# Threshold attention and its feed-forward block on one core: centring behind the masks, the last quarter product ahead of the next scores, the variance in a slot's second half

## The chip, the cores and the metric

The kernel runs on one core of a Trainium2 chip. The metric is the time on the device in microseconds (us), the median of several runs. A core has five engines that run side by side and wait for each other through semaphores: TensorE (PE in the profile, its weight loads PEld), VectorE (DVE), ScalarE (ACT), GpSimd (POOL) and SyncE (SP), which issues most transfers here.

## The reference

Eight batches, eight heads, 576 positions, head size 64. Attention keeps only scores that lie within `tau` of their row's maximum; a feed-forward block (FFN) with layer norm and a residual follows.

```python
scores = scale * q @ k.T                       # (8, 8, 576, 576)
thresh = max(scores, -1) - tau
scores = where(scores >= thresh, scores, -1e9)
attn   = exp(scores - max(scores, -1));  attn /= sum(attn, -1) + 1e-9
x      = attn @ v                              # heads side by side: (8, 576, 512)

mu  = mean(x, -1);  var = mean((x - mu) ** 2, -1)
xn  = (x - mu) / sqrt(var + 1e-6) * g_ln
out = x + relu(xn @ w_ch1) @ w_ch2             # 512 -> 2048 -> 512
```

All inputs and the output are float32.

## The kernel before

The attention of a batch is cut into 9 **slots**, 72 in all. A slot computes the scores of four blocks of 128 rows, their maxima, exponentials, masks and sums, and turns the weights over by way of DRAM; the product with the values follows a slot later. The FFN runs on 16 **groups** of 288 positions, two per batch, and fills TensorE's time between the attention's products. Every slot has four **quarters**, 0 to 3; a call can be hung on a quarter, and each quarter has a quota of FFN steps.

The heart of a slot. The engines take instructions in the order in which this loop issues them:

```python
for n in range(NS):                       # NS = 72
    scores(b, s); run(n, -1)              # TensorE -> sc[0], sc[1] in PSUM
    rest = exponentials(n)                # DVE maxima (L399), ACT exp of blocks 0 and 1 (L410)
    es, thr = next(rest)
    run(n, 0); ...; second_part(n, 0)     # quarter 0
    next(rest, None)                      # ACT exp of blocks 2 and 3
    ...                                   # transposes of the next q and k, where due
    run(n, 1); second_part(n, 1)          # quarter 1
    diags = weights(es, thr, blocks_go)   # DVE masks with row sums (L417), POOL scaling (L433)
    run_all(aside); drip(); ...
    run(n, 2); second_part(n, 2)          # quarter 2
    scr = turn_blocks(s, es)              # DVE block transposes (L498), et -> scr in DRAM
    at_quarter(n + 1, 0, ...fetch...)     # scr -> em
    at_quarter(n + 1, 3, ...values_of...) # TensorE, L542, into pv_behind
    if s in (HP, 2 * HP): group_ready(2 * b + (s > HP))
    run_all(aside); drip({nc.vector: 4, nc.gpsimd: 6}); ...
    run(n, 3); ...; second_part(n, 3)     # quarter 3
    run_all(aside); drip({nc.vector: 2, nc.gpsimd: 0})
```

`pv_behind`, where the value products go, lies behind the two score blocks in `sc[0]`, in the last of its three banks. `aside` and `drops` hold short vector work (root steps, sums, output stores) that is issued between quarters.

When a group's input is complete, three calls are hung up: its mean (a product with a matrix of 1/512), the centring, and the start of its FFN steps.

```python
def ready(g):
    if g < 2: return (24, 42)[g]
    b, t = divmod(g, 2)
    return QUARTERS * (b * SLOTS + (HP, 2 * HP)[t] + 2) + (2, 4)[t]

def group_ready(g):
    first = divmod(ready(g), QUARTERS)
    for fn in (mean_of, centre):
        at_quarter(*(divmod(ready(g) - 1, QUARTERS) if g else (first[0], -1)), fn, g)
    at_quarter(*first, lambda: queue.append(ffn_steps(g)))

def mean_of(g):
    if banks_taken[0]:
        waiting_mean.append(g)            # no bank free: the last quarter product issues it
        return
    means[g] = ps_ff.tile([128, TOK], F32, tag="ff", name="mean")
    product(means[g], lhsT=avg_sb, rhs=sums.pop(g), start=True, stop=True)

def centre(g):
    nonlocal issued, owed
    while waiting_mean:                   # draws FFN steps until the mean is out
        cost = next(queue[0])[1]
        issued += cost
        owed -= cost
    xc = centred[g] = ffn.tile([128, NK, TOK], F32, tag="xc", bufs=1, name="xc")
    for c in range(NK):                   # four DVE subtractions, L593
        nc.vector.tensor_tensor(out=xc[:, c], in0=groups[g][:, c], in1=mean, op=ALU.subtract)
```

So the first group of a batch (g even) is ready in quarter 2 of slot 6 of its batch and the second (g odd) in quarter 0 of slot 2 of the next; the mean and the centring are hung one quarter earlier. Group 1 is ready in quarter 2 of slot 1 of batch 1. The pool `ps_ff` has two banks, for all FFN products, means and variances.

The quota. `issued` counts FFN steps by cost, `owed` is what a quarter still has to issue:

```python
ROOM = (0.6, 1.0, 1.25, 0.35)

def second_part(n, i):
    at = QUARTERS * n + i
    g = sum(issued >= e for e in ends)
    left = sum(ROOM[t % QUARTERS] for t in range(at, ready(g + 1))) if g + 1 < NG else 0
    owed += (ends[g] - issued) * ROOM[i] / left if left > 0 else 8
    got = 1 if i in (0, QUARTERS - 1) else 2
    while queue and (owed >= 0.5 or got == 1 and i in (0, QUARTERS - 1)):
        got, cost = next(queue[0], (None, 0))
        ...
        issued += cost; owed -= cost
```

The steps of a group: 16 rows of four products (`p1`, 128x288, cost 1 each) with a relu after each row; on the way the square, the variance and the reciprocal root. Then, for all groups but the first, seven quarter products (`seg`, 16 steps of cost 0.5 each, two products of 128x144 per step), the last of them in the bank that the mean waits for.

```python
def first_part(g):
    for d in range(ND):                                     # ND = 16
        while d == ND - 2 and len(rooted) <= g: run_all(aside)
        p1 = ps_ff.tile([128, TOK], F32, tag="ff", name="p1")
        for c in range(NK): product(p1, ...); ... yield 1, 1
        nc.scalar.activation(hidden[:, d], p1, func=AF.Relu)            # L716
        if sq is None and d and (plain or part > 1 or d == ND // 2 - 1):
            squared = d
            sq = hidden[:, ND - NK :]
            nc.scalar.activation(sq, xc, func=AF.Square)                # L722, then 3 POOL sums
        elif sq is not None and rb is None and d >= squared + (7 if plain else 4) and (part or d == ND - NK - 1):
            var = ps_ff.tile([128, TOK], F32, tag="ff", name="var")
            product(var, lhsT=avg_sb, rhs=sq[:, 0], start=True, stop=True)
            rb = ffn.tile([128, TOK], F32, tag="rb", bufs=2, name="rb")
            nc.scalar.activation(sq[:, 2], var, func=AF.Identity, bias=eps_sb)
            aside.append(lambda: root(rb, sq[:, 2], sq[:, 3]))
            yield 1, 1

def root(y, x, t, step=0):                                  # DVE, on 128x288
    if step == 0: ... first guess (L650)
    ... three instructions of a Newton step (L654, L657, L658)
    if step < 2: aside.append(lambda: root(y, x, t, step + 1))
    else: rooted.append(y)

def second_quarters(g, rb):
    banks_taken[0] = True
    ... six segments ...
    last = segment(s4, b22)
    for _ in range(12): yield next(last)
    banks_taken[0] = False
    while waiting_mean: mean_of(waiting_mean.pop(0))
    p3 = yield from last                                    # 4 more steps, then a copy on ACT (L797)
```

Of the kernel before, what the change touches and what calls it, by code (L numbers as in the profile page):

```python
# [18 lines left out]
def kernel(  # L19
# [37 lines left out]
    NK = DM // 128  # L57
    ND = DF // 128
# [37 lines left out]
    def product(out, lhsT, rhs, **flags):  # L96


        for h in range(2):
            r = slice(64 * h, 64 * h + 64)  # L100
            nc.tensor.matmul(out[r], lhsT=lhsT[:, r], rhs=rhs, **flags)  # L101
# [480 lines left out]
        product(means[g], lhsT=avg_sb, rhs=sums.pop(g), start=True, stop=True)  # L582

    def centre(g):
        nonlocal issued, owed
        while waiting_mean:
            cost = next(queue[0])[1]
            issued += cost
            owed -= cost
        xc = centred[g] = ffn.tile([128, NK, TOK], F32, tag="xc", bufs=1, name="xc")  # L590
        mean = means.pop(g)
        for c in range(NK):
            nc.vector.tensor_tensor(  # L593
                out=xc[:, c], in0=groups[g][:, c], in1=mean, op=ALU.subtract
            )
# [4 lines left out]
    aside, stores, drops = [], [], []  # L600
# [17 lines left out]
    def run_all(calls):  # L618
        now = calls[:]
        calls.clear()  # L620
        for fn in now:
            fn()
# [23 lines left out]
    def root(y, x, t, step=0):  # L646


        if step == 0:
            nc.vector.tensor_scalar(  # L650
                out=y.bitcast(I32), in0=x.bitcast(I32), scalar1=-0.5, scalar2=float(0x5F3759DF),
                op0=ALU.mult, op1=ALU.add,
            )
        nc.vector.scalar_tensor_tensor(  # L654
            out=t, in0=y, scalar=-0.5, in1=y, op0=ALU.mult, op1=ALU.mult
        )
        nc.vector.tensor_mul(t, t, x)  # L657
        nc.vector.scalar_tensor_tensor(out=y, in0=t, scalar=1.5, in1=y, op0=ALU.add, op1=ALU.mult)  # L658
        if step < 2:
            aside.append(lambda: root(y, x, t, step + 1))  # L660
        else:
            rooted.append(y)

# [10 lines left out]
    def differences():  # L674


        flat = conversion.stage.rearrange("p a b -> p (a b)")
        flat4 = e_room[1].rearrange("p a b -> p (a b)")
        size = HM * HD * 128
        for t in (flat[:, :size], flat[:, size : 2 * size], flat4[:, :size]):  # L680
            more.append(t.rearrange("p (m d c) -> p m d c", m=HM, d=HD))
        s2, s3, s4 = more
        s1 = w2[1, 0]
        for eng, out, a, b, op in (
            (nc.gpsimd, s3, w2[0, 0], w2[1, 0], ALU.subtract),
            (nc.vector, s1, w2[1, 0], w2[1, 1], ALU.add),
            (nc.vector, s2, s1, w2[0, 0], ALU.subtract),
            (nc.gpsimd, s4, w2[0, 1], s2, ALU.subtract),
        ):
            for m in range(HM):  # L690
                for d in range(0, HD, 4):
                    at = (slice(None), m, slice(d, d + 4))
                    eng.tensor_tensor(out=out[at], in0=a[at], in1=b[at], op=op)
                    yield

    def first_part(g):


        xc = centred.pop(g)
        rb = sq = None  # L700
        plain = g == 0
        sums_of = differences() if g == 1 else iter(())
        for d in range(ND):
            while conversion.ended < 4 * (d // 4 + 1):
                yield 0, 0
            while d == ND - 2 and len(rooted) <= g:
                run_all(aside)
            p1 = ps_ff.tile([128, TOK], F32, tag="ff", name="p1")
            for c in range(NK):
                product(  # L710
                    p1, lhsT=w1_sb[c][:, d * 128 : (d + 1) * 128], rhs=xc[:, c],
                    start=(c == 0), stop=(c == NK - 1),
                )
                if c < NK - 1:
                    yield 1, 1
            nc.scalar.activation(hidden[:, d], p1, func=AF.Relu)  # L716
            next(sums_of, None)
            yield 2, 1
# [3 lines that stand above are left out]
                nc.scalar.activation(sq, xc, func=AF.Square)  # L722
                for c in range(1, NK):
                    nc.gpsimd.tensor_tensor(out=sq[:, 0], in0=sq[:, 0], in1=sq[:, c], op=ALU.add)
            elif sq is not None and rb is None and d >= squared + (7 if plain else 4) and (part or d == ND - NK - 1):

                var = ps_ff.tile([128, TOK], F32, tag="ff", name="var")
                product(var, lhsT=avg_sb, rhs=sq[:, 0], start=True, stop=True)
                rb = ffn.tile([128, TOK], F32, tag="rb", bufs=2, name="rb")
# [3 lines that stand above are left out]
        for _ in sums_of:  # L733
            pass
        return rb
# [118 lines left out]
    def ffn_steps(g):  # L854
        rb = yield from first_part(g)
        yield from (second_quarters if g else second_plain)(g, rb)
# [3 lines left out]
    QUARTERS = 4  # L860
# [5 lines left out]
    queue = []  # L866
    issued = part = now = 0
    owed = 0.0
    later_calls = {}

    def at_quarter(n, i, fn, *args):
        later_calls.setdefault((n, i), []).append((fn, args))
# [5 lines left out]
    def ready(g):  # L878

        if g < 2:  # L880
            return (24, 42)[g]
        b, t = divmod(g, 2)
        return QUARTERS * (b * SLOTS + (HP, 2 * HP)[t] + 2) + (2, 4)[t]
# [25 lines left out]

    def group_ready(g):  # L910
        first = divmod(ready(g), QUARTERS)
        for fn in (mean_of, centre):
            at_quarter(*(divmod(ready(g) - 1, QUARTERS) if g else (first[0], -1)), fn, g)
        at_quarter(*first, lambda: queue.append(ffn_steps(g)))

    conversion = Weights()
# [16 lines left out]
    for n in range(NS):  # L933
# [58 lines left out]
        if s in (HP, 2 * HP):  # L992
            group_ready(2 * b + (s > HP))
# [51 lines left out]
```

## Time and profile before

| | |
|---|---|
| time, median of 3 runs | 1425.12 us (1424.98 to 1427.36) |
| span of the profiled execution | 1420.1 us |
| granted TensorE clock | 0.993 |
| busy: PE, DVE, POOL, ACT | 94%, 67%, 43%, 32% |
| products `p` (L101) | 4096 records, 519.6 us busy |
| products `seg` (L101), all forms | 5760 records of the two large groups, 369.0 us busy |
| masks (L417) | 288 of 810 ns |
| maxima (L399) | 144 of 1351 ns |
| block transposes (L498) | 112 of 1371 ns |
| centring (L593) | 64, median 447 ns |

A group's row in the profile names line, engine, operation, output and inputs, shape and count, then busy time and the mean duration of one, then the idle time of the engine just before and what ended it. L101 is the helper `product`, so its groups go by tiles: `p` is a row of the first FFN product, `seg` a quarter product, `mean` and `var` the two averages. A product of this helper is two half matmuls, and each stands as two records, so four records are one product. `<-` after a gap names what the engine waited for. A timeline line gives start, duration (of merged instructions together), engine, line, operation, tiles, count, and in brackets the gap ahead of it.

### The profile page before, as it was taken

Reading aid. Unit: us, or ns where it says so; the run is one execution under the profiler, and the core shown is the slowest. Engines: PE = TensorE matmul, PEld = TensorE weight load, DVE = VectorE, ACT = ScalarE, POOL = GpSimd, SP = SyncE. Lnnn points to the kernel's source line nnn. Section 1 sums busy time; section 2 is a strip of 40 time slices with the busy share of each in tenths; the row PEclk is TensorE's granted clock in tenths of the full one; section 3 lists DMA queues with packets and bytes.
Section 4 is the critical chain, followed back from the end, with each engine's and each line's share of the span. In section 5 each row is a group of like instructions: output and inputs, shape, how many; then the busy total and the mean of one; then the engine's idle time right before and its main releaser. Section 6 shows DMA issues by size and latency. Waiting matters only on the chain.

```text
span 1420.1 us, 36022 instructions
## 1 busy us (share of the span) xinstructions
PE 1341.9 (94%) x15048; PEld 985.7 (69%) x15048; DVE 950.0 (67%) x1638; ACT 459.1 (32%) x923; POOL 612.0 (43%) x809
## 2 busy tenths in 40 slices
PE   4878999999999999999999999999999999999996
PEld 3655665857767595866768586776858677685866
DVE  5998958576776677666775767766675677757221
ACT  3887513232222323232232322323232322223120
POOL 2445444544534354353443544343544444434312
PEclk8999999999999999999999999999999999999998
DMA  9622456557864687557875678646875577555211
GB/s 230 170 75 84 90 134 165 156 159 154 186 148 125 164 181 169 156 141 167 182 161 137 155 156 176 153 133 167 187 163 154 142 163 174 144 134 150 68 18 18
DMA packets 466867, 205.53 MB, mean 145 GB/s; under 512 B 275024, under 2 KB 428368, under 8 KB 466704
## 3 DMA queue, kind: packets, MB, share of 16 engines
q1 hardware_dynamic: 461936, 202.64, 59.7%
q8 instruction: 118, 1.93, 0.6%
q10 hardware_dynamic: 4736, 0.59, 0.4%
q14 instruction: 45, 0.37, 0.1%
q0 software_dynamic: 32, 0.00, 0.0%
HBM read 119.41 MB, written 83.76 MB: 143 GB/s over the span
## 4 chain that ended last, share of the span: by engine, by line
PE 73%; DVE 13%; DMA 5%; ACT 3%; issue 3%; POOL 1%; SPq 1%; POOLq 0%; DVEq 0%; ACTq 0%
PE p L101 29%; PE seg L101 24%; PE sc L385 9%; PE sc L542 9%; DVE e L417 3%; DMA em<-scr 3%; DVE neg L399 3%; ACT e L410 1%; DVE xc L593 1%; DMA scr<-et 1%; DVE w L291 1%; DVE w L264 1%; DVE y L801 1%; PE mean L101 0%; PE tp L101 0%
## 5 line engine op out<-in xcount | busy, mean ns | idle before, releaser
L101 PE MATMUL p<-xc,w 128*64 128x288 f32 x4096 | 519.6, 408 | 19.7 <-ACT hidden L716 9.2
L101 PEld LDWEIGHTS p<-xc,w 128*64 128x64 f32 x4096 | 288.9, 137 | 231.2 <-ACT hidden L716 20.1
L399 DVE TENSOR_REDUCE neg<-sc 128x2 f32<-128x1152 f32 x144 | 188.7, 1351 | 209.4 <-PE sc L385 209.4
L410 ACT ACTIVATE e<-sc,neg 128x576 f32<-128x576 f32 x288 | 196.3, 742 | 244.1 <-DVE neg L399 244.1
L433 POOL TENSOR_SCALAR e<-e,den 128x576 f32<-128x576 f32 x252 | 196.3, 790 | 181.9 <-DVE den L422 181.9
L101 PE MATMUL seg<-hidden,w 128*64 128x144 f32 x3840 | 245.7, 287 | 0.0
L101 PEld LDWEIGHTS seg<-hidden,w 128*64 128x64 f32 x3840 | 235.0, 137 | 8.9 <-issue 6.3
L417 DVE SCALAR_TENSOR_TENSOR e<-sc,thr,e 128x576 f32<-128x576 f32 x288 | 222.1, 810 | 22.4 <-ACT e L410 21.9
L716 ACT ACTIVATE hidden<-p 128x288 f32<-128x288 f32 x256 | 105.4, 413 | 237.1 <-PE p L101 236.2
L403 POOL TENSOR_SCALAR thr<-neg,low_sb 128x2 f32<-128x2 f32 x144 | 42.0, 292 | 321.9 <-DVE neg L399 311.9
L385 PE MATMUL sc<-kT,qT 64*128 64x384 f32 (+3 forms) x1024 | 150.6, 425 | 21.6 <-DVE qT L345 10.1
L498 DVE STREAM_TRANSPOSE et<-e 128x1152 f32<-128x1152 f32 x112 | 152.3, 1371 | 11.5 <-POOL e L433 9.6
L385 PEld LDWEIGHTS sc<-kT,qT 64*128 64x128 f32 x1024 | 94.3, 191 | 73.2 <-issue 19.6
L542 PE MATMUL sc<-em,v_in 128*64 128x256 f32 (+1 forms) x1408 | 131.6, 330 | 10.9 <-DVE e L417 5.6
L101 PE MATMUL seg<-hidden,stage 128*64 128x144 f32 x1920 | 123.3, 286 | 0.0
L101 PEld LDWEIGHTS seg<-hidden,stage 128*64 128x64 f32 x1920 | 118.3, 137 | 3.1 <-issue 2.3
L542 PEld LDWEIGHTS sc<-em,v_in 128*64 128x64 f32 x1408 | 85.6, 137 | 47.6 <-DVE e L417 9.1
L782 POOL TENSOR_TENSOR hidden<-hidden 128x576 f32<-128x576 f32 x60 | 84.6, 1429 | 29.5 <-ACT hidden L716 19.6
L559 ACT COPY x<-sc 128x256 f32<-128x256 f32 x60 | 22.3, 372 | 213.5 <-PE sc L542 176.7
L568 POOL TENSOR_TENSOR sum<-sum,x 128x256 f32<-128x256 f32 (+1 forms) x64 | 32.3, 504 | 105.4 <-ACT x L559 102.9
L782 DVE TENSOR_TENSOR hidden<-hidden 128x576 f32<-128x576 f32 x60 | 47.9, 832 | 40.3 <-PE seg L101 37.3
L797 ACT COPY part<-seg 128x288 f32<-128x288 f32 x75 | 30.1, 401 | 115.3 <-PE seg L101 111.0
(151 smaller groups left out, 1204.8 us busy)
## 6 DMA issues: line engine op xcount, KB each, us to landing
scr<-et SPq DMA_DIRECT2D x252, 288.0 KB, 4.6
em<-scr SPq DMA_DIRECT2D x63, 1024.0 KB, 5.9
out_dram<-ot SPq DMA_DIRECT2D x256, 36.0 KB, 2.7
q_in<-in_q_dram SPq DMA_DIRECT2D x124, 72.0 KB, 5.2
k_in<-in_k_dram SPq DMA_DIRECT2D x120, 72.0 KB, 3.2
v_in<-in_v_dram SPq DMA_DIRECT2D x64, 128.0 KB, 4.5
rest<-scr SPq DMA_DIRECT2D x63, 128.0 KB, 5.9
w<-in_moe_w_ch_dram SPq DMA_DIRECT2D x10, 512.0 KB, 6.0
```

The costliest lines, as they stand in the source:

```text
L101: nc.tensor.matmul(out[r], lhsT=lhsT[:, r], rhs=rhs, **flags)
L385: nc.tensor.matmul(sc[h][64 * i : 64 * i + 64 if s == HP else 128, at : at + n], lhsT=ql[r] if s == HP else qT[r, half, j * 128 : (j + 1) ...
L399: nc.vector.tensor_reduce(out=neg[:, i], in_=pairs[h], axis=AXL.X, op=ALU.max, negate=True,)
L403: nc.gpsimd.tensor_scalar(out=thr[:, i], in0=neg[:, i], scalar1=-1.0, scalar2=low_sb, op0=ALU.mult, op1=ALU.add,)
L410: nc.scalar.activation(es[:, i], blocks[i], func=AF.Exp, bias=neg[:, i : i + 1])
L417: nc.vector.scalar_tensor_tensor(out=es[:, i], in0=blocks[i], scalar=thr[:, i : i + 1], in1=es[:, i], op0=ALU.is_ge, op1=ALU.mult, accum_o ...
L433: nc.gpsimd.tensor_scalar(out=es[:, i], in0=es[:, i], scalar1=den[:, i : i + 1], scalar2=1.0, op0=ALU.mult, op1=ALU.mult,)
L498: nc.vector.transpose(et[:, :, 64 * h : 64 * h + 64].rearrange("p n (j c) -> p j n c", j=2), es[:, 2 * h : 2 * h + 2].rearrange("p j (n c) ...
L542: nc.tensor.matmul(dst[64 * h : 64 * h + 64], lhsT=vt[:, c, h, :] if c < J else vr[:, h, :], rhs=pick(em[:, c] if c < J else er, hp, h), s ...
L568: nc.gpsimd.tensor_tensor(out=sums[g][:, cols], in0=x[:, 0, cols] if c == 1 else sums[g][:, cols], in1=x[:, c, cols], op=ALU.add,)
L716: nc.scalar.activation(hidden[:, d], p1, func=AF.Relu)
L782: eng.tensor_tensor(out=out[at], in0=in0[at], in1=in1[at], op=op)
```

## The change

Three parts, all of them about the order in which instructions are issued.

- The centring of a group that becomes ready in quarter 2 (a batch's first group, and group 1) is hung on quarter 2 itself, which is issued behind the masks. The mean stays where it was. A group that becomes ready in quarter 0 is centred where it was.
- The steps that `centre` draws in order to get the mean out are no longer taken off `owed`. It is meant to let the quarter issue the rest of the old group's last quarter product ahead of the next scores.
- The variance of all groups but the first is taken in quarter 2 or 3 only, and one row sooner after the square; the first two root steps are issued together.

```diff
     def centre(g):
-        nonlocal issued, owed
+        nonlocal issued
         while waiting_mean:
-            cost = next(queue[0])[1]
-            issued += cost
-            owed -= cost
+            issued += next(queue[0])[1]
...
-        if step < 2:
-            aside.append(lambda: root(y, x, t, step + 1))
+        if step == 0:
+            root(y, x, t, 1)
+        elif step == 1:
+            aside.append(lambda: root(y, x, t, 2))
         else:
             rooted.append(y)
...
-            elif sq is not None and rb is None and d >= squared + (7 if plain else 4) and (part or d == ND - NK - 1):
-
+            elif sq is not None and rb is None and (
+                d >= squared + (7 if plain else 3) and part > (0 if plain else 1)
+                or d == ND - NK - 1
+            ):
...
     def group_ready(g):
         first = divmod(ready(g), QUARTERS)
-        for fn in (mean_of, centre):
-            at_quarter(*(divmod(ready(g) - 1, QUARTERS) if g else (first[0], -1)), fn, g)
+        before = divmod(ready(g) - 1, QUARTERS) if g else (first[0], -1)
+        at_quarter(*before, mean_of, g)
+        at_quarter(*(first if g and first[1] else before), centre, g)
         at_quarter(*first, lambda: queue.append(ffn_steps(g)))
```

## The prediction

> **What bounds the kernel now.** I read the busy shares first, then the list of what TensorE (PE) waited for, then stretches of the timeline of one batch.
>
> ```profile
> PE 1341.9 (94%) x15048; PEld 985.7 (69%) x15048; DVE 950.0 (67%) x1638; ACT 459.1 (32%) x923; POOL 612.0 (43%) x809
> ...
> PE 73%; DVE 13%; DMA 5%; ACT 3%; issue 3%; POOL 1%; SPq 1%; POOLq 0%; DVEq 0%; ACTq 0%
> ```
>
> TensorE is the bound: 94% busy, 78 us idle, of which the start of the program takes a good part. VectorE (DVE) is busy two thirds of the time, so its order matters only where TensorE ends up waiting for it. No multiplication is added or removed, so all that the change can win is TensorE's idle time. The list of its waits (total us, times, longest):
>
> ```profile
> PE sc L385 <- DVE qT L345: 10.1, 1, 10.1
> PE p L101 <- ACT hidden L716: 9.2, 11, 2.8
> PE p L101 <- ACT part L797: 8.7, 14, 0.7
> PE sc L542 <- DVE e L417: 5.6, 7, 0.9
> PE sc L542 <- DMA em<-scr: 4.6, 7, 1.1
> PE sc L385 <- ACT x L559: 1.5, 6, 0.3
> ```
>
> The 10.1 us is the first load. The others come once or twice per batch, and three stretches of batches 4 and 5 show where. First, slot 6 of batch 4, where the batch's first group is centred (slots are numbered within a batch; L593 centring, L417 masks, L542 value products):
>
> ```profile
> 777.47 0.66 PE L101 MATMUL mean<-sum,avg_sb 128*64 128x288 f32 x4
> 777.96 1.15 PE L101 MATMUL seg<-hidden,e 128*64 128x144 f32 x16
> 778.17 1.55 DVE L593 TENSOR_TENSOR xc<-x,mean 128x288 f32<-128x288 f32 x4 [3.60 <-PE mean L101]
> 779.23 0.40 ACT L797 COPY part<-seg 128x288 f32<-128x288 f32 x1 [2.90 <-PE seg L101]
> 779.64 0.81 DVE L417 SCALAR_TENSOR_TENSOR e<-sc,thr,e 128x576 f32<-128x576 f32 x1
> ...
> 779.68 0.71 PE L101 MATMUL p<-xc,w 128*64 128x288 f32 x4 [0.57 <-ACT part L797]
> ...
> 781.25 0.87 PE L542 MATMUL sc<-em,v_in 128*64 128x256 f32 x6 [0.86 <-DVE e L417]
> ```
>
> DVE stood idle 3.60 us for the mean although the masks could have run, and the masks then released the value products 0.86 us late. Second, TensorE in slots 1 and 2 of batch 5 (scores of slot 2 at 862.70):
>
> ```profile
> 862.03 0.41 PE L101 MATMUL seg<-hidden,e 128*64 128x144 f32 x4
> 862.70 2.21 PE L385 MATMUL sc<-kT,qT 64*128 64x384 f32 x16 [0.25 <-ACT x L559]
> 864.84 0.71 PE L101 MATMUL seg<-hidden,e 128*64 128x144 f32 x8
> ...
> 868.18 1.19 PE L101 MATMUL p<-xc,w 128*64 128x288 f32 x8 [0.68 <-ACT part L797]
> ```
>
> The last quarter product is cut by the scores; its copy out of PSUM then sits on ScalarE (ACT) behind two exponentials (the copy starts at 867.73), and the new group's second product waits 0.68 us for that bank. Third, slot 8 of batch 4 (scores at 805.35):
>
> ```profile
> 810.84 8.95 PE L101 MATMUL p<-xc,w 128*64 128x288 f32 x72 [0.70 <-ACT hidden L716]
> ...
> 815.54 0.29 DVE L650 TENSOR_SCALAR rb<-hidden 128x288 int32<-128x288 int32 x1
> 815.72 1.66 POOL L433 TENSOR_SCALAR e<-e,den 128x576 f32<-128x576 f32 x2 [0.19 <-DVE den L422]
> 815.87 0.90 DVE L654 SCALAR_TENSOR_TENSOR hidden<-rb 128x288 f32<-128x288 f32 x1
> ...
> 821.05 2.63 DVE L498 STREAM_TRANSPOSE et<-e 128x1152 f32<-128x1152 f32 x2
> ```
>
> The variance product stands in the slot's second quarter, while the relu before it is stuck behind exponentials: 0.70 us. The whole root, 10 instructions, then runs from 815.54 to 821.05, ahead of the block transposes that feed the transfer for slot 0 of the next batch.
>
> [...] masks with ready inputs stood 3.60 us behind a centring without its mean. [...] The value products write other columns of `sc[0]` than the masks read[...], and the trace shows them waiting (0.86 us). [...] The root's L654 took 0.90 us beside the POOL scaling of 1.66 us, and 0.46 us later without it. [...] TensorE's end times are modelled; so I compare starts, which make each wait some 0.17 us longer than the gap shown (0.86 becomes 1.03 against the usual spacing of these products).
>
> **Part 1, centring of a batch's first group behind the masks.** It adds nothing. From the scores' start (769.64) the two maxima are done at 774.57, that is +4.93. Four masks at 0.81 us and two reciprocals at 0.17 take some 3.4 us, so they end near +8.4, or 778.0. The mean arrives at 778.13. The masks therefore fit almost exactly into DVE's idle stretch, and centring stays at about 778.2; the first product after it (779.68, held by the bank's copy and not by centring) shouldn't move. The masks end at 778.0 instead of 782.9. The wait "PE sc L542 <- DVE e" disappears: **5.6 us** in its 7 places. The block transposes (783.12 to 786.05 now) go to after centring, about 779.8, 3.3 us earlier, and so does the transfer for slot 7. The 0.57 us on the bank's copy stays.
>
> **Part 2, the quota.** One unit of FFN work is a product of 128x288, 4 records, 0.485 us from start to start; a step of a quarter product is half a unit, 0.243 us. I followed `second_part` by hand. Before: `centre` draws steps until the mean is out and takes them off `owed`, so the quarter's quota comes out short by as much. In slot 6 that leaves 3 steps for the third quarter and then one product, before the values; the trace has just this (16 records, 4 of them in the second quarter, then 4). Without the subtraction the four remaining steps follow the mean at once. The third quarter gets the new group's normal quota, 11 products, and 5 follow the values: 16 before the next scores instead of 8. Slot 6 becomes some 8 x 0.485 = 3.9 us longer, less the wait, and slots 7 and 8 shorter. For the second groups (slot 1) all 3 remaining steps stand between the values and the scores of slot 2. Their 0.73 us covers the copy of x (the 0.25 us wait, where only one step stood), and the copy of the bank comes ahead of the exponentials (0.68 us). In six places: 6 x 0.68 + 1.5 = **5.6 us**. Of the 8.7 us for part, 4.6 stays: the 7 first groups and the tail, where no scores intervene.
>
> **Part 3, variance in the second half, two root steps at once.** By the same count a first group is squared after its second row of products, in slot 6, and its variance moves from slot 8's second quarter to slot 7's third. For a second group it moves from slot 3's second quarter to the third. Exponentials are over by then, so 7 waits of 0.70 go: 4.9 us, less an allowance of 0.07 us each for the place where the variance product now stands (the second group's, at 888.20 in batch 5, shows no gap of 0.2 us behind it): **4.4 us**. Root steps 1 and 2 are 7 instructions, about 3 us, now behind the transposes. In slot 8 the transposes start near 815.7 plus the scaling, about 816, instead of 821.05. With part 1 this clears the transfer waits of slots 7 and 0 (0.98, 0.41, 1.03, 0.40 of the 4.6 us; the other three are in batch 1): **2.8 us**.
>
> **Sum.** 5.6 + 5.6 + 4.4 + 2.8 = 18.4 us of shown gaps. At 0.17 us more for each of some 30 waits, +5. New small waits, an estimate of a half microsecond per batch: -3.5. Net 20 us: 1425.1 - 20 = **1405 us**.
>
> **Rivals.** *A: the end of the masks is no longer the limit, and centring becomes it.* If the masks run late (a maximum or exponential held up), xc comes after 779.7 and the new group's products wait, 1 to 2 us in each of 7 groups. For it: masks' end and mean are only 0.1 us apart, and centring writes four chunks at 0.45 us each. Against: TensorE is held until 779.68 by the copy, by which time in this estimate all four are written. It would leave 1413 to 1418. *B: the second half fills up.* In slot 7 DVE gets seven root instructions, the stores' transposes and the last root step (some 8 us) after the block transposes at about +11.7, while the next scores come at +16.6 and want the maxima at +18.7. Squaring on POOL (3 x 0.82) now precedes the finishing sums. If these delay maxima and masks, the value products wait again: 1410 to 1420, and over 1425 only if it happens in every batch by 3 us. Against it: the masks end about +8.4 and are wanted only at the values, about +13. *C: more falls.* Adding up the starts, each of batches 2 to 7 shows some 6.7 us beyond the usual spacing of its products. If all goes but the bank's copy (0.75) and the steps between scores and other products (1.8), some 4 us of it are won per batch, 28 in seven: 1397.
>
> **Range and chances.** C sets the low end, A with B the high one: **1397 to 1418**. Over 2% faster means below 1396.6, which needs all idle time of the steady part but the copies: 0.08. Within 2%: 0.90. Slower by over 2%: 0.02, as nothing adds work.
>
> **What would show it.** Right: "PE sc L542 <- DVE e L417" gone from the waits; centring with no idle time or under 1 us before it in slot 6; "PE p <- ACT part" at 7 or 8 times; "PE sc <- ACT x" gone; the 0.70 us of slot 8 gone; TENSOR_REDUCE still following its scores by 0.2 us. Wrong: a new wait of p for xc (A), maxima well after the scores (B), or waits for em in other slots.

## The result, and the profile after

| | before | after |
|---|---|---|
| time, median | 1425.05 us (1424.95 to 1427.36) | 1437.09 us (1433.54 to 1439.88) |
| ratio, 95% interval | | 1.0079 (1.0051 to 1.0107) |
| span of the profiled execution | 1420.1 us | 1438.1 us |
| TensorE clock | 0.993 | 0.981 |

The change made the kernel 0.8% slower where 1.4% faster was forecast. The traced execution before took 1421.85 us and the one after 1439.88, so sums over the traces differ by some 18 us where the medians differ by 12.0. The first page line and the list of what TensorE waited for, after the change:

```profile
PE 1354.7 (94%) x15048; PEld 996.9 (69%) x15048; DVE 931.3 (65%) x1638; ACT 459.9 (32%) x923; POOL 607.5 (42%) x809
```

```profile
PE sc L542 <- DMA em<-scr: 25.1, 7, 5.1
...
PE p L101 <- ACT hidden L716: 5.6, 3, 2.8
PE p L101 <- ACT part L799: 4.6, 8, 0.6
...
PE p L101 <- DVE xc L591: 1.9, 1, 1.9
```

Nearly every forecast about waits came true: the masks and x are gone from the list, `part` stands at 8 times and 4.6 us. One line went the other way: the value products wait 25.1 us for the transfer `em`, where it was 4.6. TensorE's busy time also rose by 13 us with the same 15048 instructions, at a granted clock of 0.981 instead of 0.993. The slot in which the first group is centred (slot 6 of batch 4, scores at 781.27), as the timeline has it after the change:

```profile
789.10 0.66 PE L101 MATMUL mean<-sum,avg_sb 128*64 128x288 f32 x4
...
789.87 1.52 DVE L591 TENSOR_TENSOR xc<-x,mean 128x288 f32<-128x288 f32 x4
...
791.31 5.56 PE L101 MATMUL p<-xc,w 128*64 128x288 f32 x44 [0.57 <-ACT part L799]
791.31 2.63 DVE L498 STREAM_TRANSPOSE et<-e 128x1152 f32<-128x1152 f32 x2
...
796.69 1.90 PE L542 MATMUL sc<-em,v_in 128*64 128x256 f32 x16
```

Centring follows the masks without idle time, the first product starts 10.04 us after the scores, exactly as before, and 11 products (44 records) stand ahead of the values; only the first of them waits, 0.57 us for the bank's copy, as before. To see where the time went I added up the lengths of the slots, from one start of the scores to the next, over batches 2 to 7 (slot 8 of batch 7, which holds the tail, left out). Two experiments told below are beside them:

| slot | 0 | 1 | 2 | 3 | 4 | 5 | 6 | 7 | 8 | sum |
|---|---|---|---|---|---|---|---|---|---|---|
| before, us | 108.2 | 115.3 | 116.6 | 112.6 | 95.3 | 107.1 | 101.9 | 112.4 | 97.2 | 966.6 |
| after | 143.0 | 110.3 | 108.2 | 112.6 | 93.8 | 108.6 | 120.6 | 100.9 | 85.3 | 983.3 |
| e4, quota docked | 117.3 | 113.4 | 109.8 | 112.6 | 93.8 | 108.6 | 97.4 | 108.2 | 93.8 | 954.9 |
| e5, stores spread | 106.1 | 110.3 | 110.3 | 112.6 | 93.8 | 108.6 | 120.6 | 100.9 | 85.4 | 948.6 |

Slots 1 to 8 together won 18.1 us. Slot 0 alone lost 34.8 us. TensorE in slot 0 of batch 5, and then of batch 4, after the change:

```profile
852.23 3.68 PE L542 MATMUL sc<-em,v_in 128*64 128x256 f32 x16 [2.84 <-DMA em<-scr]
855.69 1.07 PE L542 MATMUL sc<-rest,v_rest 128*64 128x256 f32 x4
```

```profile
688.58 1.95 PE L542 MATMUL sc<-em,v_in 128*64 128x256 f32 x16 [2.84 <-DMA em<-scr]
690.36 0.60 PE L542 MATMUL sc<-rest,v_rest 128*64 128x256 f32 x4
```

The same wait of 2.84 us, but in batch 5 the same 16 records then take 3.68 us instead of 1.95. The windows view gives TensorE's granted clock for 25 us around each (batch 4, then 5), third column from the end:

```profile
668.00:693.00 25.00, 22.16 (x298) 18.97 (x296) 11.43 (x20) 4.88 (x10) 12.11 (x13) 1.00 0.84 170
835.00:860.00 25.00, 22.16 (x266) 18.58 (x264) 11.44 (x20) 4.09 (x8) 11.57 (x13) 0.86 0.84 176
```

In batch 5 the clock record has half speed for 6.83 us from 851.45 on, and that slot is 23.70 us long against 20.74 in batch 4: 2.96 us for the same wait. All of the six batches but batch 4 show it. So slot 0 divides up: the waits for `em` are 3.75, 5.14, 2.84, 2.84, 4.61 and 2.97, together 22.2 us, where four gaps made 2.3 us before: +19.8. With its wait taken off, slot 0 of batch 4 is 17.90 us long, and those of the other five are 2.97, 2.15, 2.96, 2.41 and 2.93 us longer than that: +13.4 beside the half clock. Together 33.2 of the 34.8 us; where the other 1.6 lie is not shown.

Why `em` is late stands on SyncE's queue. From the fetch of slot 8 to that of slot 0 of the next batch (batches 4 and 5), first before, then after; start, duration of the issuing, count (after the change with the last of VectorE's block transposes):

```profile
807.01 0.45 SPq L513 DMA_DIRECT2D em<-scr  x1
...
808.06 9.64 SPq L639 DMA_DIRECT2D out_dram<-ot  x16
...
823.70 3.90 SPq L504 DMA_DIRECT2D scr<-et  x4
...
833.17 0.45 SPq L513 DMA_DIRECT2D em<-scr  x1
```

```profile
821.44 0.45 SPq L513 DMA_DIRECT2D em<-scr  x1
...
822.49 10.77 SPq L637 DMA_DIRECT2D out_dram<-ot  x16
...
830.06 1.38 DVE L498 STREAM_TRANSPOSE et<-e 128x1152 f32<-128x1152 f32 x1 [0.17 <-POOL e L433]
...
833.37 2.01 SPq L116 DMA_DIRECT2D q_in<-in_q_dram  x4
835.42 2.12 SPq L116 DMA_DIRECT2D k_in<-in_k_dram  x4
837.63 3.94 SPq L504 DMA_DIRECT2D scr<-et  x4
...
846.22 0.45 SPq L513 DMA_DIRECT2D em<-scr  x1
```

After the change the block transposes end at 831.44, but `scr` goes out at 837.63: SyncE issued in order and was still at 16 output stores (10.77 us) and 8 loads of q and k (2.01 and 2.12 us). From one `em` to the other it takes 26.2 us before (0.5 of them waiting for the transposes, 1.4 standing until the first `em` had landed) and 24.8 after (1.2 standing in the same way). It did not get slower; the slots got shorter. Slot 8 fell from 19.44 to 17.07 us, and its own `em` was already 1.6 us later against the scores (+3.2 instead of +1.7), so the next one is issued 10.95 us after slot 0's scores instead of 8.38. In the kernel before there was no slack: in all six batches the values of slot 0 start 0.14 us behind the landing of `em`.

### The profile page after: what moved, and what is told of

It is laid out like the page before. It is cut to its first block, busy times and chain, and to the rows that moved or that the text cites. A ratio compares the mean times of both kernels' runs of the same rounds, so it can differ in the third digit from the quotient of the medians.

```text
span 1438.1 us, 35976 instructions
## 1 busy us (share of the span) xinstructions
PE 1354.7 (94%) x15048; PEld 996.9 (69%) x15048; DVE 931.3 (65%) x1638; ACT 459.9 (32%) x923; POOL 607.5 (42%) x809
## 4 chain that ended last, share of the span: by engine, by line
PE 77%; DMA 7%; DVE 6%; SPq 5%; ACT 2%; issue 2%; POOL 1%; POOLq 0%; DVEq 0%; ACTq 0%
PE p L101 31%; PE seg L101 25%; PE sc L542 10%; PE sc L385 9%; DMA em<-scr 3%; DVE e L417 2%; SPq L116 1%; DVE neg L399 1%; SPq L504 1%; SPq L134 1%; DMA rest<-scr 1%; DMA scr<-et 1%; DMA v_in<-in_v_dram 1%; PE tp L101 1%; SPq L130 1%
## 5 line engine op out<-in xcount | busy, mean ns | idle before, releaser
L101 PEld LDWEIGHTS seg<-hidden,w 128*64 128x64 f32 x3840 | 235.4, 137 | 11.5 <-issue 7.7
L385 PE MATMUL sc<-kT,qT 64*128 64x192 f32 (+3 forms) x1024 | 149.0, 424 | 19.8 <-DVE qT L345 10.1
L542 PE MATMUL sc<-em,v_in 128*64 128x256 f32 (+1 forms) x1408 | 141.2, 347 | 25.1 <-DMA em<-scr 25.1
L498 DVE STREAM_TRANSPOSE et<-e 128x1152 f32<-128x1152 f32 x112 | 153.1, 1374 | 12.6 <-POOL e L433 10.8
L542 PEld LDWEIGHTS sc<-em,v_in 128*64 128x64 f32 x1408 | 90.2, 145 | 62.8 <-DMA em<-scr 27.0
L101 PEld LDWEIGHTS seg<-hidden,stage 128*64 128x64 f32 x1920 | 121.2, 140 | 4.7 <-issue 4.2
```

Source lines behind the costliest of these rows:

```text
L385: nc.tensor.matmul(sc[h][64 * i : 64 * i + 64 if s == HP else 128, at : at + n], lhsT=ql[r] if s == HP else qT[r, half, j * 128 : (j + 1) ...
L498: nc.vector.transpose(et[:, :, 64 * h : 64 * h + 64].rearrange("p n (j c) -> p j n c", j=2), es[:, 2 * h : 2 * h + 2].rearrange("p j (n c) ...
L542: nc.tensor.matmul(dst[64 * h : 64 * h + 64], lhsT=vt[:, c, h, :] if c < J else vr[:, h, :], rhs=pick(em[:, c] if c < J else er, hp, h), s ...
```

## The experiments

Theory Q, formed from this: the forecast gains are real, but moving eight products from slots 7 and 8 into slot 6 shortens just the slots in which SyncE's queue is full, and the fetch for slot 0 falls behind. Rivals: V, the later variance or the root behind the transposes costs; D, the transfers themselves are slower; C, the clock falls because TensorE is busier. Against D the two traces speak already: in slot 0 of batches 2 to 7 `em` takes 5.7 to 6.7 us from issue to landing before and 5.7 to 6.6 after, but is issued 7.22 to 8.38 us behind the scores before and 10.95 to 13.27 after.

**e1: the third part alone**, on the kernel before (the diff's changes to the variance's condition and to `root`).

> The kernel before with the third part alone (variance in quarter 2 or 3, two root steps at once). Theory Q (the gains came as worked out, but the shorter slots 7 and 8 leave SyncE's in-order queue behind, so that the transfer em of slot 0 is issued some 3 us later and TensorE waits): the quota of the first groups is untouched here, slots 7 and 8 keep some 18 and 19 us, so no new wait in slot 0: 1415 to 1422. Rival V (the root, now behind the block transposes in slot 7, or the later variance, is what costs): slot 0 waits 3 to 5 us as in the changed kernel, 1435 or more. Rival C (TensorE's clock falls because it is kept busier): a clock under 0.993 without waits.

Measured: 1423.32 us, ratio 0.9989 (0.9976 to 1.0003). No loss, so V falls. Hardly a gain either: in the traced execution slot 8 became 7.0 us shorter in five batches, but slot 7 became 6.6 and slot 0 7.9 us longer in six, and the waits for `em` are 9.8 us instead of 4.6. Even this small shift met the queue.

**e2: the first part alone** (only `group_ready` changed).

> The kernel before with the first part alone (centring of a first group behind the masks). Since the mean is then drawn by the quota and not by the centring, this alone already moves the quota: 16 products before the scores of slot 7 instead of 8. Theory Q: slots 7 and 8 at about 17 us, em of slot 0 issued near +11 us, waits of 2 to 5 us there and half a clock after them: 1433 to 1445. Rival V: no variance moved, so no new wait: about 1415.

Measured: 1460.85 us, ratio 1.0260 (1.0225 to 1.0295), slower than forecast: waits for `em` of 36.2 us, slot 0 at 153.5 us in the sum of six. Here the root also stays ahead of the transposes, so `em` of slot 8 is issued at +5.5 us and that of slot 0 at +12.6 (batch 5).

**e3: half of the stores earlier**, in the changed kernel:

```diff
+        if n >= SLOTS:
+            for _ in range(min(2, len(stores))):
+                stores.pop(0)()
         second_part(n, 3)
```

> The changed kernel, with up to two of a group's four output stores (8 of 16 transfers) issued in quarter 3 of the slot in which they are made (slot 7) instead of all after the fetch in slot 8. Theory Q: scr of slot 8 is issued some 4 to 5 us earlier, right behind the block transposes, em of slot 0 near +6 to +7 us, the wait in slot 0 gone and the half clock with it: 1400 to 1407. Rival D (the transfers themselves are slower, as the DMA engines are shared): em still lands at +15 or later, 1430 to 1440. Rival V or C: 1430 to 1440.

Measured: 1433.52 us, ratio 1.0057 (1.0043 to 1.0071): a miss. `em` of slot 8 moved from +3.2 to +7.2, and that of slot 0 stayed at +10.9. There was no free time in which SyncE could have sent them. By its interval the run is not told apart from the changed kernel. It doesn't separate Q from D; it says that order alone does not help within one slot.

**e4: the slots' lengths restored**, in the changed kernel, SyncE's order untouched:

```diff
+        if g and first[1]:
+            at_quarter(*first, dock)        # owed -= 5.5
         at_quarter(*first, lambda: queue.append(ffn_steps(g)))
```

> The changed kernel with 5.5 units taken off the quota when a first group is centred, so that 8 products stand before the scores of slot 7 as in the kernel before, and slots 7 and 8 are as long as there. SyncE's order is untouched. The variance of a first group falls back into slot 8 by this. Theory Q: em of slot 0 is issued near +8 us, waits there of 0 to 1 us as before, no half clock: 1408 to 1418. Rival V or D: as the changed kernel, 1430 to 1440.

Measured: 1410.62 us, ratio 0.9903 (0.9873 to 0.9932). With slots 7 and 8 long again, slot 0 falls from 143.0 to 117.3 us. The transfers, their order and the centring are those of the changed kernel. C falls: TensorE does the same work in less time, at a granted clock of 0.994 (0.981 in the changed kernel). V is not tested here, since the variance of a first group stands in slot 8 again. Not all of the loss is gone: `em` of slot 0 is issued at +9.4 (batch 5; forecast: near +8), and the waits in slot 0 are 0.4 to 2.2 us, more than forecast.

**e5: the stores spread over slots**, in the changed kernel; slots stay short:

```diff
-        run_all(stores)
+        for _ in range(min(1, len(stores)) if n >= SLOTS else len(stores)):
+            stores.pop(0)()
         second_part(n, 0)
```

> The changed kernel, with one output store (4 transfers) sent per slot instead of a group's four (16) at once, all still on SyncE. What the run before it showed: sending half of them earlier only moved the fetch of slot 8 back, because SyncE has no free time there; the work has to be spread. Theory Q (SyncE's queue of slots 7 to 0 is full): slot 8 has some 6 us less ahead of scr, so scr goes out right behind the block transposes and em of slot 0 near +6 us; no wait, no half clock there: 1399 to 1408. Slots 1 and 2 get 4 transfers more each and may wait a little. Rival D (transfers slow by sharing the DMA engines): em lands late all the same, 1425 or more.

Measured: **1402.91 us** (1402.6 to 1403.4), ratio 0.9844 (0.9819 to 0.9869), the forecast of the change within 2.1 us. SyncE in slot 8 of batch 4:

```profile
803.21 2.27 SPq L637 DMA_DIRECT2D out_dram<-ot  x4
...
812.74 4.04 SPq L504 DMA_DIRECT2D scr<-et  x4
...
821.19 0.45 SPq L513 DMA_DIRECT2D em<-scr  x1
```

From `em` (802.16) to `em` 19.0 us instead of 24.8, and slot 0 is at 106.1 us. Waits for `em` are down to 3.9 us. That the same bytes move while the wait goes speaks against D, too. The slack is small: in batch 5 `em` lands 0.3 and 0.9 us ahead of its use in slots 0 and 1, and in slot 2 TensorE waits 1.77 us for it.

**e6: the stores from ScalarE**, in the changed kernel:

```diff
-            nc.sync.dma_start(
+            nc.scalar.dma_start(
                 out=out[b, t * TOK : ...
```

> The changed kernel, with the output stores issued by ScalarE instead of SyncE: the same bytes at about the same time, on another engine's queue. Theory Q: SyncE loses some 8 to 11 us of issuing in slot 8, em of slot 0 near +6 us, its wait gone. ScalarE issues 16 transfers ahead of the second pair of exponentials, so masks in slots 8 and 3 are some us later: 1400 to 1415. Rival D: the same transfers share the DMA engines as before, so slot 0 waits as long as before: 1430 to 1440.

Measured: 1552.91 us, ratio 1.0896 (1.0867 to 1.0926). Half right: slot 0 is at 106.1 us, as in e5, with all stores at once, as Q has it. By itself this doesn't decide against D, since slot 8 grew from 17.1 to 29 or 30 us and so left more time for the fetch. That is because ScalarE pays (its row of slot 8 of batch 4, then TensorE's):

```profile
874.43 10.22 ACTq L637 DMA_DIRECT2D out_dram<-ot  x14
884.70 0.41 ACT L716 ACTIVATE hidden<-p 128x288 f32<-128x288 f32 x1 [9.82 <-DMA q_in<-in_q_dram]
```

```profile
885.16 2.19 PE L101 MATMUL p<-xc,w 128*64 128x288 f32 x8 [9.18 <-ACT hidden L716]
```

The relu of the running product stands behind these 14 issues and two before them. I had counted exponentials and masks as delayed, and not the relu, without which TensorE has no free bank: 119.6 us in 17 such waits. For one transfer the issuing was the small part (0.45 us for `em`, and 5.8 us, the median after the change, until it landed); 16 of them in a row ahead of something urgent were what mattered.

**e7: the second part alone** (only `centre` changed).

> The kernel before with the second part alone (the steps drawn by the centring are not taken off the quota; centring still ahead of the masks). By the count, slots 6 to 8 get the same products as in the changed kernel. Theory Q: em of slot 0 late by 3 us or more, waits of 3 to 6 us with a half clock, as with the first part alone: 1435 to 1462. Rival (the place of the centring is what costs): 1415 to 1422.

Measured: 1458.31 us, ratio 1.0231 (1.0203 to 1.0259): as Q has it, waits of 35.5 us for `em`. The place of the centring is not the cause. In its list of waits the masks no longer hold up the values, though centring still stands ahead of them.

**e8: e5, and the loads of v behind the fetch**:

```diff
-            load_v((n + 2) // SLOTS * HP + (n + 2) % SLOTS)
+            at_quarter(n + 1, 0, load_v, (n + 2) // SLOTS * HP + (n + 2) % SLOTS)
```

> As e5, and besides the loads of v (4 transfers a slot, needed two slots later) are issued behind the fetch of the next slot instead of ahead of it. Theory Q: em is then issued as soon as scr has landed, in slots 0, 1 and 2 some 2 to 4 us earlier than in e5; if e5 still shows waits there, they go: 1397 to 1404. If e5 shows none, the same time as e5. Rival D: no better than e5.

Measured: 1441.38 us, ratio 1.0116 (1.0081 to 1.0151): wrong. `em` of slot 0 is issued at +6.2 (batch 5), but in slots 1 and 2 at +9.3 and +11.5, and slot 2 sums to 138.3 us. Ahead of `em` SyncE now stands idle until `scr` has landed (4.0 us in slot 0 of batch 5, from 839.52 to 843.54), a stretch that the loads of v had filled, and behind `em` it meets the same work plus those loads.

**e9: the spreading alone**, on the kernel before (the edit of e5).

> The kernel before with one output store per slot, nothing else. If the gain of e5 were that of the spreading alone, this would be near 1403. Theory Q: the long slots 7 and 8 of the kernel before nearly cover SyncE's queue already; only its waits for em in slots 7 and 0 (some 3 us in all) can go: 1419 to 1424.

Measured: 1424.12 us, ratio 0.9989 (0.9974 to 1.0004). The gain of e5 is not that of its edit alone. Of the waits for `em`, which by Q should shrink, the trace shows 8.7 us instead of 4.6.

**e10, e11, e12: e5 without one part each**, for what each part is worth once the queue no longer hides it.

> e5 without the third part (variance and root as before). By the count the variance of a first group stands in slot 7's second quarter, with the relu behind exponentials: 7 waits of 0.7 us come back, and the root stands ahead of the block transposes in slots 7 and 3, which have some us to spare. Third part worth 4 to 5 us, as in the prediction's sum: 1406 to 1409. If the move of the root matters more (em late again), over 1412.

Measured: 1415.74 us, ratio 0.9928 (0.9901 to 0.9955). The third part is worth 12.8 us against e5, where 4 to 5 were forecast. Waits on the relu rise by 5.0 us (10.6 against 5.6 in the list), those on `em` by 5.0 (8.9 against 3.9): with the root ahead of the transposes `em` of slot 8 is issued at +5.5 instead of +3.3, and slot 2 grows by 5.6 us. That the one leads to the other is argued, not shown.

> e5 without the first part (centring ahead of the masks, but with the quota not docked). The prediction gave 5.6 us to the first part, for the value products' wait on the masks in slot 6. But eight more products now stand ahead of those value products, so they should come after the masks in any case: 1402 to 1405, that is nothing lost. If the prediction's term holds by itself: 1408 to 1410.

Measured: 1402.56 us, ratio 0.9832 (0.9800 to 0.9863). Beside the other parts the first is worth nothing that shows within the spread of these runs (1399.2 to 1406.4 us).

> e5 without the second part (steps drawn by the centring are taken off the quota). First groups keep the changed quota through the first part; second groups go back to a last quarter product cut by the scores: 6 waits of 0.68 on part and 6 of 0.25 on x come back, some 0.9 us each and 0.17 more by the starts: 1408 to 1411. If the second part only moves time about, 1402 to 1405.

Measured: 1407.15 us, ratio 0.9869 (0.9842 to 0.9895). The second part is worth 4.2 us; the waits on `part` are back at 8.7 us in 14 places and those on x at 1.3 us in 6.

## Why the prediction was wrong

**Part 1.** Its times were right to 0.3 us: masks' end at +8.7 us from the scores (worked out: +8.4), centring at +8.6, transposes from +10.0. Rival A came true once only, in group 1 (the 1.9 us for xc). But its 5.6 us were counted twice: the 8 more products that part 2 puts ahead of the values let the masks end in time anyway (e7, e11). Beside part 2 the term is 0. (The prediction's list of waits leaves out its longest line, 11.0 us of the scores behind the masks; those lie in batch 0, and it is 10.8 us after the change.)

**Part 2.** The count held: 16 products before the scores of slot 7, slot 6 at 20.1 us, slots 7 and 8 at 16.8 and 17.1, the waits of the second groups gone. I noted that slots 7 and 8 would be "shorter" and took it as moving time about. It was the cause of the loss.

**Part 3.** The 0.70 us waits left, and the list of waits on the relu fell from 9.2 to 5.6 us. Rival B did not come: the root fits behind the transposes (in slot 7 of batch 4 it starts at 812.96, the last step ends at 819.19, and the maxima wait for the scores). For the relu the 4.4 us were about right: 5.0 us of such waits come back in e10. The rest of the 12.8 us there is no part of that term; 5.0 us of it are waits for `em`.

**The step that failed** is the last of part 3: "With part 1 this clears the transfer waits of slots 7 and 0", worth 2.8 us. It let a transfer follow the end of its transposes. For slot 7 this was right: its `em` now lands 6.1 to 6.8 us ahead of its use. For slot 0 the transfer follows SyncE's queue: in the kernel before, `scr` of slot 8 went out at 823.70, 0.02 us after the transposes, but right behind the loads of k, so two limits stood within half a microsecond of each other. The prediction used SyncE's row of the timeline for none of this, and no rival named it; only its last sign of being wrong, waits for `em` in other slots, points there. In place of +2.8 us stands -34.8 us in slot 0. With the queue relieved and the rest unchanged, the kernel takes 1402.9 us, and a gain of the forecast size is there. That the size agrees is luck, for the split is another: e10 to e12 give the parts 12.8 (third), 0 (first) and 4.2 us (second), 17.0 in all, when each is taken out of the full set, where the prediction's gaps gave 4.4, 5.6 and 5.6 and 2.8 for the transfers.

**The clock.** Nothing in the prediction allowed for it. After the change the clock record has five stretches at half speed in slot 0, in batches 2, 3, 5, 6 and 7, each of 6.83 us, and each begins during the wait for `em` (in batch 5 2.06 us into it). In batch 4 there is none. The wait is 2.84 us in batches 4 and 5 alike, and in the 25 us around it TensorE is busy for 22.16 us in both; why the granted clock is 0.86 there in batch 5 and 1.00 in batch 4 is not shown. The four runs of the changed kernel differ in time as in clock, from 1433.5 us at 0.987 to 1439.9 at 0.981.

## What to carry to other kernels

When work moves between stages without being added, ask of each stage that gets shorter what else was using its length; here it was an in-order issuing queue that appears nowhere in the busy shares. Follow a transfer back to its issue and read what its queue did just before, even where the wait that ended last names the data. And take out one part at a time from the full change, too: a gain that two parts can each bring is easily counted twice.

## What the runs showed that was not expected

Issuing was slow enough to be a bound: the 16 stores of slot 8 kept SyncE for 9.64 us in the kernel before (1.4 of them standing until `em` had landed), four writes of `scr` for 3.90 us, and in e6 14 stores kept ScalarE for 10.22 us, any standing included. Some transfers were held until `em` had landed. In slot 8 of batch 4 after the change `em` (issued at 821.44) lands at 827.23, and the seventh store goes out at 827.24, 1.75 us behind the start of the sixth; in the same slot of the kernel before, `em` lands at 812.89 and the seventh store goes out at 812.91. The list of what SyncE waited for, before and after (stores), then in e5 (loads of q and k):

```profile
SPq L639 <- DMA em<-scr: 19.2, 14, 2.2
```

```profile
SPq L637 <- DMA em<-scr: 19.4, 14, 2.1
```

```profile
SPq L116 <- DMA em<-scr: 19.4, 24, 1.3
```

What ties these transfers to `em` is not shown. And where the clock halved, a wait of under 3 us cost as much again: slot 0 of batch 5 is 2.96 us longer than that of batch 4, with a wait of 2.84 us in both.
